# A new head, load order and matmul order for a gated SSM/FFN mix on one Trainium2 core

## The chip, the cores and the metric

The program runs on one core of a Trainium2 chip. A core has five engines that run their own instruction queues and meet only through semaphores: TensorE (PE in the profile, with PEld for its weight loads), VectorE (DVE), ScalarE (ACT), GpSimd (POOL) and SyncE (SP), which here issues nearly all DMAs. Matmul results land in eight PSUM banks. The metric is the device time of one execution in microseconds (us), lower being better. Three executions of the kernel before took 150.77, 152.63 and 154.89 us (median 152.63).

## The reference

Everything is computed for one sequence of 2048 tokens with 448 features, in bf16:

```
g   = sigmoid(sum(x * gate_w))                       # one gate per token
# branch a: a diagonal complex state-space layer, 448 states
dt  = exp(log_dt);  L = exp(dt * (Lambda_re + i Lambda_im))
Bu  = x @ (((L - 1) / Lambda)[:, None] * B).T        # complex
h_t = L * h_{t-1} + Bu_t                             # over 2048 steps
a   = 2 * Re(h @ C.T) + x * Dskip
# branch b: a feed-forward layer, 448 -> 1792 -> 448
b   = silu(x @ w1) @ w2
out = g * a + (1 - g) * b
```

## The kernel before

**Tiling.** The 2048 tokens are cut into 4 stretches of 512 (`tc` = 0 to 3) and 16 blocks of 128 (`tb`). Features are held transposed in `xT` (128 partitions, 4 column blocks; the last block starts at 320, so its upper 64 rows are new). For stretch 0, `xT` is made on TensorE from `xnat` (L409); for the others by transposing DMAs (L365).

**The scan without complex numbers.** Rotating by the phase of each state turns the complex recurrence into a real one with decay `rc`. For each stretch `bu_pair` and `bu_last` give `U` (real and imaginary parts in 7 slots of 128 lanes, with the two halves of slot 3 exchanged into slot 7). `lanes(tc)` is VectorE's part: PA = U·COS, PB = U·SIN (two instructions), PA += PB, then 7 `tensor_tensor_scan` into `Gf` (order of slots 3, 0, 4, 1, 5, 2, 6), each turned into bf16 `Gb` by ScalarE (L636), then Gb·SIN, Gb·COS and their difference `H[tc % 2]`. Six small VectorE instructions (L642 to L646 and `gin`) carry the state on to the next stretch. COS and SIN are tables over 512 positions, made once: GpSimd multiplies positions by `ph` into `Gf` (L464), VectorE takes off the nearest integer (L450, L453), ScalarE computes Sin, Abs and Sin again (L470 to L476), VectorE copies the second half (L478, L479).

**The matmuls.** `F1(tc, k)` is a pair of column blocks of `x @ w1`, `BU(tc, k)` a pair of slots of `Bu`. A pair uses products of 64 rows, two at a time: a "begin" of 8 for the pair, and an "end" of 6, which is issued only after the begin of the next pair (`step`, `close`). So a pair is 14 products and holds 2 banks until its two results are moved out by ScalarE: `aT` (SiLU, L658) or `U` (L587; for stretch 0 half of them by VectorE, L585). `F2(tb)` is 14 products of 128 rows with `w2`, moved out by ScalarE to `Tb` (L672). `C(tb)` is the readout, 7 products of 128 rows of `H` with `CP`, moved out by VectorE to `ot` (L696) after `tf` (L687). `bu_last` (L607) and `gates` (L732) also use 128 rows, and so do the transposes of `B` into `BT` (L533) and of `C` (`readout_weights`, L709).

**What sets the order.** TensorE runs in the order in which the source calls `F1`, `BU`, `F2`, `C` and the rest. For the other engines a planner (`Plan.order`) picks at each point the instruction that can start first by written-down costs, and by `prio` (lower first) among those that can start at once; it also gives out the banks. The result is one fixed list for each engine: an instruction that waits holds up all behind it on its engine.

**DMAs on SP, in order:** x of stretch 0, four pieces of B, three of w1, the transposing loads of stretch 1, w2, four pieces of C, the transposing loads of stretches 2 and 3, Dskip, x of stretches 1 to 3; then the exchanges of slot 3 (`swapped`) and the results.

Of the kernel before, what the change touches and what calls it, by code (L numbers as in the profile page):

```python
# [46 lines left out]
class Plan:  # L47
# [54 lines left out]
    def order(self):  # L102
# [28 lines left out]
        while len(done) < len(ops):  # L131
# [20 lines left out]
            if o.sem is not None:  # L152
                free[o.eng] = t + 0.35
                pipe = max(pipe, t + 1.5) + o.bytes / 260e3
                o.end = pipe + 0.4
            else:
                extra = 0.0
                if o.eng == "pe":
                    extra = self.SWITCH if o.rows != rows else 0.0
                    rows = o.rows  # L160
                free[o.eng] = o.end = t + o.cost + extra
# [3 lines left out]
            for tk in o.ps_w:  # L165
                b = min((x for x in range(8) if holder[x] is None), key=lambda x: (banks[x], x))
                tk.bank = b
                tk.left = tk.users
                holder[b] = tk
# [88 lines left out]
def bass_gated_mix__ssm_conv_s5__dense_activation_silu__prompt_kernel(nc, A_x, A_Lambda_re, A_Lambda_im, A_B_re, A_B_im, A_C_re, A_C_im,  # L258
               A_log_dt, A_Dskip, B_x, B_w1, B_w2, gate_w, out):
    with ExitStack() as ctx:  # L260
# [64 lines left out]
        def sem():  # L325
            _s[0] += 1
            return E(nc.semaphore(name=f"d{_s[0]}"))
# [22 lines left out]
        def load(q, dst, src, name, nbytes, prio):  # L350
            P.add(q, lambda e: e.dma_start(dst, src), [], [name], 0.3, prio, sem(), nbytes)
# [5 lines left out]
        def load_x(tc, prio):  # L357
            load("sp", xnat[:, 4 * tc:4 * tc + 4, :], x2[tc * CH:(tc + 1) * CH, :].rearrange("(b p) d -> p b d", p=128),
                 f"xn{tc}", CH * 896, prio)

        def load_xt(tc, n, prio):

            rows = slice(tc * CH, (tc + n) * CH)
            for k, (o, c) in enumerate(((slice(0, 3), slice(0, 384)), (slice(3, 4), slice(320, 448)))):
                P.add("sp", lambda e, o=o, c=c: e.dma_start_transpose(xT[:, o, rows], x2[rows, c]), [],  # L365
                      [f"xT{t}{k}" for t in range(tc, tc + n)], 1.2, prio + k, sem(), n * CH * (1100, 500)[k])
# [3 lines left out]
        load("sp", Bnat[0:64, 3, :], A_B_re[384:448, :], "Bn1", 64 * 896, 2)  # L370
        load("sp", Bnat[64:128, 3, :], A_B_im[384:448, :], "Bn2", 64 * 896, 3)
        load("sp", Bnat[:, 4:7, :], A_B_im[0:384, :].rearrange("(p s) d -> p s d", s=3), "Bn3", 384 * 896, 4)
        load("sp", w1s[:, 0:3, :], B_w1[0:384, :].rearrange("(b p) f -> p b f", p=128), "w1a", 384 * 3000, 5)
        load("sp", w1s[0:64, 3, 0:896], B_w1[320:384, 0:896], "w1b", 64 * 1500, 6)
        load("sp", w1s[64:128, 3, :], B_w1[384:448, :], "w1c", 64 * 3000, 7)
        load_xt(1, 1, 8)
        load("sp", w2s[:, :, :], B_w2.rearrange("(fb p) d -> p fb d", p=128), "w2", F_FF * 896, 10)
# [4 lines left out]
        load_xt(2, 2, 16)  # L382
        load("sp", dsk[:, :],
             A_Dskip.rearrange("(o n) -> o n", o=1).partition_broadcast(128).rearrange("p o n -> p (o n)"),
             "dsk", 128 * 896, 18)
        for tc in range(1, NCH):
            load_x(tc, 18 + tc)
# [14 lines left out]
        for n, blocks in enumerate(((0, 1), (2, 3))):  # L402
            tk = Ps()

            def mm(pe, tk=tk, blocks=blocks):
                for q, i in enumerate(blocks):
                    for b in range(4):
                        o = (q * 4 + b) * 128
                        r = pe.transpose(bk16(tk)[:, o:o + 128], xnat[:, b, XCOL[i]:XCOL[i] + 128], ident[:, :])  # L409
                return r  # L410
            P.add("pe", mm, ["xn0", "ident"], [tk], 0.6)
            dst = xT[:, blocks[0]:blocks[0] + 2, 0:CH]
            src = lambda tk=tk: bk16(tk)[:, :].rearrange("p (q n) -> p q n", q=2)
            if n == 0:
                DVE(lambda e, src=src, dst=dst: e.tensor_copy(dst, src()), [tk], ["xT00"], 0.7, 2)
            else:
                ACT(lambda e, src=src, dst=dst: e.activation(dst, src(), AF.Copy), [tk], ["xT01"], act_cost(1024), 1)

        def xr(tc):
            return [f"xT{tc}{k}" for k in range(2)]  # L420
# [38 lines left out]
        FR = [Gf[:, 2 * h:2 * h + 2, :] for h in range(2)]  # L459
        wk = [Gf[:, 4, :], Gf[:, 5, :]]  # L460
        for b in range(4):
            h, q = b // 2, b % 2
            dst = Gf[:, b, :]
            POOL(lambda e, b=b, dst=dst: e.tensor_single_scalar(dst, itf[:, :], ph[:, b:b + 1], ALU.mult),  # L464
                 ["itf", "ph"], [f"Gf{b}"], 0.65)
            DVE(nearest(wk[q], dst), [f"Gf{b}"], [f"Gf{4 + q}"], dve_cost(512, 2), 3)
            DVE(minus(dst, dst, wk[q]), [f"Gf{b}", f"Gf{4 + q}"], [f"Gf{b}"], dve_cost(512), 3)
        for h in range(2):
            n = 2 if h == 0 else 1
            ACT(lambda e, h=h, n=n: e.activation(SIN[:, 2 * h:2 * h + n, :], Gf[:, 2 * h:2 * h + n, :], AF.Sin, scale=TURN),  # L470
                [f"Gf{2 * h + k}" for k in range(n)] + ["tbl"], [f"SIN{2 * h + k}" for k in range(n)], act_cost(n * 512), 5)
            if h == 1:
                ACT(lambda e: e.activation(SIN[:, 3, :], Gf[:, 3, :], AF.Sin, scale=sturn[:, :]),  # L473
                    ["Gf3", "sturn", "tbl"], ["SIN3"], act_cost(512, 1), 5)
            ACT(lambda e, h=h: e.activation(FR[h], FR[h], AF.Abs), ["tbl"], [f"Gf{2 * h}", f"Gf{2 * h + 1}"], act_cost(1024), 5)
            ACT(lambda e, h=h: e.activation(COS[:, 2 * h:2 * h + 2, :], FR[h], AF.Sin, bias=hpi[:, :], scale=-TURN),  # L476
                [f"Gf{2 * h}", f"Gf{2 * h + 1}", "hpi", "tbl"], [f"COS{2 * h}", f"COS{2 * h + 1}"], act_cost(1024, 1), 5)
# [45 lines left out]
        def b_transposes(slots, reads, h, to_act):  # L523
# [15 lines left out]
            if to_act:  # L539
                ACT(lambda e: e.activation(dst, src(), AF.Copy), [tk], [name], act_cost(256 * n), 2)  # L540
            else:
                DVE(lambda e: e.tensor_copy(dst, src()), [tk], [name], 0.1 + 0.00058 * 256 * n, 2)

        RE, LAST, IM = (0, 1, 2), (3,), (4, 5, 6)
        b_transposes(RE, ["Bn0"], 0, False)
        b_transposes(RE, ["Bn0"], 1, True)
        bre = ["BT0_0", "BT1_0"]
        bim = ["BT0_4", "BT1_4"]
        b3 = ["BT0_3", "BT1_3", "BT3z"]
# [39 lines left out]
        def bu_pair(tc, k):  # L589
            sa, sb_ = ((0, 1), (4, 2), (5, 6))[k]  # L590
# [4 lines left out]
            return BT, tc, 128 * sa, 128 * sb_, (bre, bre + bim, bim)[k], evict  # L595

        def swapped(t, tn, prio):
            for k, (p, q) in enumerate(((0, 64), (64, 0))):
                P.add("sp", lambda e, p=p, q=q: e.dma_start(t[p:p + 64, 7, :], t[q:q + 64, 3, :]),
                      [f"{tn}3"], [f"{tn}7{'ab'[k]}"], 0.3, prio, sem(), 65536)  # L600

        def bu_last(tc):
# [7 lines left out]
            P.add("pe", mm, b3 + xr(tc), [tk], 0.87)  # L610
# [11 lines left out]
        def lanes(tc):  # L622
# [16 lines left out]
            if tc + 1 < NCH:  # L639
                last = Gf[:, :, CH - 1]  # L640
                gfn = [f"Gf{s}" for s in range(7)]
                DVE(lambda e: e.tensor_tensor(k1[:, :], last, CC[:, :], ALU.mult), gfn + ["CC"], ["k1"], 0.2, pr)  # L642
                DVE(lambda e: e.tensor_tensor(k2[:, 0:3], Gf[:, 4:7, CH - 1], SS[:, 0:3], ALU.mult), gfn + ["SS"], ["k2a"], 0.2, pr)
                DVE(lambda e: e.tensor_tensor(k2[:, 4:7], Gf[:, 0:3, CH - 1], SS[:, 4:7], ALU.mult), gfn + ["SS"], ["k2b"], 0.2, pr)
                DVE(lambda e: e.tensor_tensor(k2[0:64, 3:4], Gf[64:128, 3, CH - 1:CH], SX[64:128, :], ALU.mult), gfn + ["SX"], ["k2c"], 0.2, pr)
                DVE(lambda e: e.tensor_tensor(k2[64:128, 3:4], Gf[0:64, 3, CH - 1:CH], SX[0:64, :], ALU.mult), gfn + ["SX"], ["k2d"], 0.2, pr)  # L646
                DVE(minus(gin[:, :], k1[:, :], k2[:, :]), ["k1", "k2a", "k2b", "k2c", "k2d"], ["gin"], 0.2, pr)
# [7 lines left out]
        def ffn1_pair(tc, k):  # L655
# [4 lines left out]
            return w1s, tc, 128 * k, 896 + 128 * k, ["w1a", "w1b", "w1c"], evict  # L660
# [21 lines left out]
        def readout(tb):  # L682
# [16 lines left out]
            P.add("sp", lambda e: e.dma_start(out2[t0:t0 + 128, :], ot[tb % 3][:, :]), [f"ot{tb % 3}"], [], 0.3, 1,  # L699
# [59 lines left out]
        b_transposes(LAST, ["Bn1", "Bn2"], 0, False)  # L759
        b_transposes(LAST, ["Bn1", "Bn2"], 1, False)  # L760
        DVE(lambda e: e.memset(BT[0:64, 3, 384:512], 0.0), ["BT1_3"], ["BT3z"], 0.2, 2)
        b_transposes(IM, ["Bn3"], 0, False)
        b_transposes(IM, ["Bn3"], 1, True)
# [5 lines left out]
        F1(1, 0)  # L769
        gates(1)  # L770
        lanes(0)
        skip(0)
        F1(1, 1)
        F2(0, 1)
        BU(1, 0)
        bu_last(1)
        BU(1, 1, 2)
        F1(1, 2)
        readout_weights(0)
        readout_weights(1)  # L780
        F2(2)
        F1(1, 3, 4)
        readout_weights(2)
        readout_weights(3)
        F2(3)
        F1(1, 5, 6)
        lanes(1)
        skip(1)
        BU(2, 0)
        gates(2)  # L790
        gates(3)
        bu_last(2)
        BU(2, 1, 2)
        F1(2, 0)
        F2(4)
        C(0, 1)
        F2(5)
        F1(2, 1, 2, 3)
        C(2, 3)
        F2(6, 7)  # L800
# [3 lines left out]
        F1(2, 4)  # L804
        BU(3, 0)
        bu_last(3)
        BU(3, 1, 2)
        F1(2, 5, 6)
        F1(3, 0)
        F2(8)  # L810
        C(4, 5)
        F2(9)
        F1(3, 1, 2, 3)
        F2(10)
        C(6, 7)
        F2(11)
        F1(3, 4, 5, 6)
        lanes(3)
        close()
        C(8, 9, 10, 11)  # L820
        F2(12, 13, 14, 15)
# [36 lines left out]
```

## Time and profile before

| What | us |
|---|---|
| median of three executions | 152.63 |
| the profiled execution itself | 152.47 |
| its span (first to last instruction) | 150.4 |
| PE busy / DVE busy / ACT busy / POOL busy | 139.3 / 123.3 / 83.6 / 21.7 |
| first matmul (transposes of x) | 4.17 |
| first pair of BU(0, 0) begins | 8.86 |
| first F1 begins | 16.33 |
| first PA = U·COS begins on VectorE | 31.33 |
| last matmul of the chain ends | 147.53 |

The span is 2.07 us shorter than the time of the same execution; what lies around it is start and end of the program. The profile lists for each engine the busy time, for each group of instructions their mean duration, and for idle time the instruction that ended it. The chain that ended last is followed back from the last instruction. A busy PE need not be a fast PE: the duration of a matmul record has some pipeline time in it, so costs of matmuls are read here as the distance from one group to the next in the chain, divided by the number of matmuls.

### The profile page before, as it was taken

How to read it: one execution, taken by the hardware profiler on the slowest of the kernel's cores; microseconds unless marked ns; L12 is line 12 of the kernel's file. 1: busy time of each engine (PE TensorE's matmuls, PEld its weight loads, DVE VectorE, ACT ScalarE, POOL GpSimd, SP SyncE). 2: the span in 40 equal slices, each digit the busy share in tenths (PEclk: the TensorE clock that was granted, in tenths of full speed). 3: DMA queues.
4: the chain of work that ended last, by engine and by line, in shares of the span. 5: the costliest groups of instructions: out<-in, count | busy, mean ns of one | idle time of the engine just before them, and what ended most of it. 6: DMA issues, size and time to landing. Idle time of an engine off the chain costs nothing.

```text
span 150.4 us, 2663 instructions
## 1 busy us (share of the span) xinstructions
PE 139.3 (93%) x1055; PEld 68.0 (45%) x1059; DVE 123.3 (82%) x153; ACT 83.6 (56%) x153; POOL 21.7 (14%) x52
## 2 busy tenths in 40 slices
PE   0877999999999999999999999969999999999992
PEld 0734454454345544445445534435445444555450
DVE  0359935089999998998998999998999998799772
ACT  3272999871897768576282156894163069241300
POOL 7189930040000000730000000000000000000000
PEclk9999999999999999999999999999999999999999
DMA  4999999974110000001200000010100001210012
GB/s 159 305 294 183 287 318 128 199 238 165 35 39 2 0 0 4 20 15 35 65 0 31 31 0 25 14 35 0 61 4 0 31 31 35 65 61 2 0 45 80
DMA packets 16644, 11.43 MB, mean 76 GB/s; under 512 B 7924, under 2 KB 15928, under 8 KB 16632
## 3 DMA queue, kind: packets, MB, share of 16 engines
q1 hardware_dynamic: 16624, 11.27, 30.1%
q8 instruction: 8, 0.13, 0.4%
q14 instruction: 4, 0.03, 0.1%
q10 hardware_dynamic: 8, 0.00, 0.0%
HBM read 6.94 MB, written 1.84 MB: 58 GB/s over the span
## 4 chain that ended last, share of the span: by engine, by line
PE 87%; ACT 4%; DVE 4%; DMA 2%; issue 1%; DVEq 0%
PE ps L558 40%; PE ps L668 25%; PE ps L693 14%; DMA xnat<-in_A_x_dram 2%; PE ps L607 2%; PE ps L533 2%; DVE H L620 1%; DVE PA L620 1%; PE ps L409 1%; ACT aT L658 1%; PE ps L709 1%; PE ps L732 1%; ACT BT L540 1%; ACT Gb L636 1%; DVE ot L696 0%
## 5 line engine op out<-in xcount | busy, mean ns | idle before, releaser
L668 PE MATMUL ps<-w2s,aT 128*128 128x448 bf16 x224 | 44.2, 353 | 1.2 <-ACT aT L658 1.2
L558 PE MATMUL ps<-xT,w1s 64*128 64x512 bf16 x392 | 45.0, 376 | 0.0
L658 ACT ACTIVATE aT<-ps 128x512 bf16<-128x512 f32 x56 | 30.3, 596 | 8.0 <-PE ps L558 8.0
L668 PEld LDWEIGHTS ps<-w2s,aT 128*128 128x128 bf16 x224 | 21.5, 98 | 22.3 <-ACT aT L658 2.1
L558 PEld LDWEIGHTS ps<-xT,w1s 64*128 64x128 bf16 x392 | 18.5, 94 | 23.5 <-issue 2.2
L672 ACT ACTIVATE Tb<-ps,g 128x448 bf16<-128x448 f32 x16 | 10.1, 633 | 33.1 <-PE ps L668 31.3
L633 DVE TENSOR_TENSOR_SCAN Gf<-rc,gin,PA 128x512 f32<-128x512 f32 x21 | 25.2, 1262 | 0.0
L558 PE MATMUL ps<-xT,BT 64*128 64x512 bf16 x168 | 21.0, 388 | 2.0 <-ACT BT L540 1.0
L693 PE MATMUL ps<-CP,H 128*128 128x448 bf16 x112 | 22.2, 353 | 0.2 <-DVE H L620 0.2
L636 ACT ACTIVATE Gb<-Gf 128x512 bf16<-128x512 f32 x28 | 17.1, 630 | 4.5 <-DVE Gf L633 4.4
L587 ACT ACTIVATE U<-ps 128x512 bf16<-128x512 f32 x25 | 14.3, 596 | 6.1 <-PE ps L558 5.6
L693 PEld LDWEIGHTS ps<-CP,H 128*128 128x128 bf16 x112 | 10.7, 98 | 11.2 <-DVE H L620 0.7
L696 DVE SCALAR_TENSOR_TENSOR ot<-ps,g,tf 128x448 bf16<-128x448 f32 x16 | 10.9, 683 | 5.8 <-PE ps L693 5.2
L558 PEld LDWEIGHTS ps<-xT,BT 64*128 64x128 bf16 x168 | 8.2, 95 | 12.6 <-DVE phk L450 1.2
L687 DVE SCALAR_TENSOR_TENSOR tf<-xnat,g,Tb 128x448 f32<-128x448 bf16 x16 | 10.6, 678 | 0.5 <-ACT Tb L672 0.3
L738 POOL TENSOR_SCALAR g<-th 128x4 f32<-128x4 f32 x4 | 4.3, 1064 | 39.0 <-ACT th L737 39.0
L620 DVE TENSOR_TENSOR PB<-U,SIN 128x2048 bf16<-128x2048 bf16 (+1 forms) x8 | 8.4, 1085 | 1.3 <-ACT SIN L473 1.3
L620 DVE TENSOR_TENSOR PB<-Gb,SIN 128x1536 bf16<-128x1536 bf16 (+1 forms) x8 | 8.6, 1080 | 0.1
L620 DVE TENSOR_TENSOR H<-PA,PB 128x3584 bf16<-128x3584 bf16 x4 | 8.1, 2024 | 0.1
L620 DVE TENSOR_TENSOR PA<-U,COS 128x3584 bf16<-128x3584 bf16 x4 | 8.1, 2023 | 0.1
L620 DVE TENSOR_TENSOR PA<-PA,PB 128x3584 bf16<-128x3584 bf16 x4 | 8.1, 2024 | 0.1
L620 DVE TENSOR_TENSOR PA<-Gb,COS 128x3584 bf16<-128x3584 bf16 x4 | 8.1, 2018 | 0.0
(92 smaller groups left out, 92.5 us busy)
## 6 DMA issues: line engine op xcount, KB each, us to landing
xnat<-in_A_x_dram SPq DMA_DIRECT2D x4, 448.0 KB, 5.0
out_dram<-ot SPq DMA_DIRECT2D x16, 112.0 KB, 1.7
w2s<-in_B_w_dram SPq DMA_DIRECT2D x1, 1568.0 KB, 10.0
w1s<-in_B_w_dram SPq DMA_DIRECT2D x1, 1344.0 KB, 9.1
Gb<-Gb SPq DMA_DIRECT2D x8, 64.0 KB, 1.9
Tb<-in_A_C_re_dram SPq DMA_DIRECT2D x1, 392.0 KB, 10.4
U<-U SPq DMA_DIRECT2D x6, 64.0 KB, 2.0
Tb<-in_A_B_re_dram SPq DMA_DIRECT2D x1, 336.0 KB, 4.0
```

Of the source, the lines that this page charges most:

```text
L558: r = pe.matmul(bk(tk), w[p0:p0 + 64, k, c0:c0 + 128], xT[p0:p0 + 64, k, xc:xc + CH], start=(start and i == 0), stop=(not start and i == 2))
L587: ACT(lambda e: e.activation(U[:, s, :], bk(tk), AF.Copy), [tk], [f"U{s}"], act_cost(512), 4)
L620: return DVE(lambda e: e.tensor_tensor(o, a, b, op), r, w, dve_cost(n, 2), prio)
L633: DVE(lambda e, s=s, b=b, init=init: e.tensor_tensor_scan(Gf[:, s, :], rc[:, b:b + 1].to_broadcast([128, CH]), PA[:, s, :], init, ALU.mult ...
L636: ACT(lambda e, s=s: e.activation(Gb[:, s, :], Gf[:, s, :], AF.Copy), [f"Gf{s}"], [f"Gb{s}"], act_cost(512), 4)
L658: ACT(lambda e, tk=tk, fb=fb: e.activation(aT[tc % 2][:, fb, :], bk(tk), AF.Silu), [tk, "tbl"], [f"aT{tc % 2}_{fb}"], act_cost(512), 3)
L668: r = pe.matmul(bk(tk)[:, 0:D_MOD], aT[tc % 2][:, fb, o:o + 128], w2s[:, fb, :], start=(fb == 0), stop=(fb == NFB - 1))
L672: ACT(lambda e, tk=tk: e.activation(Tb[:, tb, :], bk(tk)[:, 0:D_MOD], AF.Copy, scale=g1[:, tb:tb + 1]), [tk, f"g1_{tc}"], [f"Tb{tb}"] + [f ...
L687: DVE(lambda e: e.scalar_tensor_tensor(tf[tb % 2][:, :], xnat[:, tb, :], g[:, tb:tb + 1], Tb[:, tb, :], ALU.mult, ALU.add), [f"xn{tc}", f" ...
L693: r = pe.matmul(bk(tk)[:, 0:D_MOD], Ht[:, s, o:o + 128], CP[:, s, :], start=(s == 0), stop=(s == NSLOT - 1))
L696: DVE(lambda e, tk=tk: e.scalar_tensor_tensor(ot[tb % 3][:, :], bk(tk)[:, 0:D_MOD], g[:, tb:tb + 1], tf[tb % 2][:, :], ALU.mult, ALU.add), ...
L738: POOL(lambda e: e.tensor_scalar(g[:, c], th[:, c], 0.5, 0.5, ALU.mult, ALU.add), [f"th{tc}"], [f"g_{tc}"], 0.2, 9)
```

## The change

- **Head.** VectorE zeroes part of `PB`, and TensorE multiplies it by itself 15 times (256 columns each) before the transposes of x, and twice more between two groups of B transposes. Nobody reads the results. `xT` of stretch 0 is moved out in three pieces instead of two. B is transposed in slot groups (0, 1), (4, 5, 6) and (2, 3) instead of (0, 1, 2), (3) and (4, 5, 6), and the pairs of BU are (0, 1), (4, 5), (6, 2) instead of (0, 1), (4, 2), (5, 6).
- **Loads.** The second large piece of B comes second. w1 comes in ten pieces: the columns for k < 3 first, then the rest. w2 goes ahead of the transposing loads of stretch 1. The transposing loads of stretches 2 and 3, Dskip and the later x wait for the exchange of `Gb` slot 3 of stretch 0.
- **Tables.** ScalarE instead of GpSimd makes two of the four blocks of `Gf`; Abs moves from ScalarE to VectorE (as max(x, -x)); the Sin instructions get `prio` 2, ahead of SiLU's 3.
- **Carries.** Four of the six small instructions for each stretch move from VectorE to GpSimd.
- **Phases.** In each stretch all pairs of 64 rows come together, and then all work of 128 rows; C and F2 alternate block by block. Before, the two kinds changed 25 times from 13.31 us on; in the new order they change 11 times from the first pair on.
- The planner's costs for DMA issue and its bookkeeping of banks are altered too, which changes the lists of ScalarE and VectorE.

```diff
         load("sp", Bnat[:, 0:3, :], A_B_re[0:384, :].rearrange("(p s) d -> p s d", s=3), "Bn0", 384 * 896, 1)
-        load("sp", Bnat[0:64, 3, :], A_B_re[384:448, :], "Bn1", 64 * 896, 2)
-        load("sp", Bnat[64:128, 3, :], A_B_im[384:448, :], "Bn2", 64 * 896, 3)
-        load("sp", Bnat[:, 4:7, :], A_B_im[0:384, :].rearrange("(p s) d -> p s d", s=3), "Bn3", 384 * 896, 4)
-        load("sp", w1s[:, 0:3, :], B_w1[0:384, :].rearrange("(b p) f -> p b f", p=128), "w1a", 384 * 3000, 5)
-        load("sp", w1s[0:64, 3, 0:896], B_w1[320:384, 0:896], "w1b", 64 * 1500, 6)
-        load("sp", w1s[64:128, 3, :], B_w1[384:448, :], "w1c", 64 * 3000, 7)
-        load_xt(1, 1, 8)
-        load("sp", w2s[:, :, :], B_w2.rearrange("(fb p) d -> p fb d", p=128), "w2", F_FF * 896, 10)
+        load("sp", Bnat[:, 4:7, :], A_B_im[0:384, :].rearrange("(p s) d -> p s d", s=3), "Bn3", 384 * 896, 2)
+        load("sp", Bnat[0:64, 3, :], A_B_re[384:448, :], "Bn1", 64 * 896, 3)
+        load("sp", Bnat[64:128, 3, :], A_B_im[384:448, :], "Bn2", 64 * 896, 4)
+        for h, (c0, c1) in enumerate(((0, 384), (384, 896))):
+            w = w1s[:, :, :].rearrange("p b (q f) -> p b q f", q=2)
+            for b in range(3):
+                load("sp", w[:, b, :, c0:c1], B_w1[128 * b:128 * b + 128, :].rearrange("p (q f) -> p q f", q=2)[:, :, c0:c1],
+                     f"w1{h}{b}", 128 * 4 * (c1 - c0), 5 + h)
...
+        load("sp", w2s[:, :, :], B_w2.rearrange("(fb p) d -> p fb d", p=128), "w2", F_FF * 896, 8)
+        load_xt(1, 1, 9, (3.0, 5.0))
...
-        load_xt(2, 2, 16)
...
+        def late_loads():
+            load_xt(2, 2, 16, (6.0, 1.4), ["Gb7a", "Gb7b"])
...
+        DVE(lambda e: e.memset(PB[:, 0, :], 0.0), [], ["PB0"], 0.2, 0)
+
+        def idle(n):
+            tk = Ps()
...
+                for _ in range(n):
+                    r = pe.matmul(ps[:, tk.bank, 0:256], PB[:, 0, 0:128], PB[:, 0, 0:256], start=True, stop=True)
+                return r
+            P.add("pe", mm, ["PB0"], [tk], 0.107 * n)
+
+        idle(15)
...
-                ACT(lambda e, src=src, dst=dst: e.activation(dst, src(), AF.Copy), [tk], ["xT01"], act_cost(1024), 1)
+                ACT(lambda e: e.activation(xT[:, 2, 0:CH], bk16(tk)[:, 0:CH], AF.Copy), [tk], ["xT01"], act_cost(512), 1)
+                DVE(lambda e: e.tensor_copy(xT[:, 3, 0:CH], bk16(tk)[:, CH:2 * CH]), [tk, "xT01"], ["xT02"], 0.42, 2)
...
+            if b < 2:
+                ACT(lambda e, b=b, dst=dst: e.activation(dst, itf[:, :], AF.Copy, scale=ph[:, b:b + 1]),
+                    ["itf", "ph"], [f"Gf{b}"], act_cost(512, 1), 2)
+            else:
+                POOL(lambda e, b=b, dst=dst: e.tensor_single_scalar(dst, itf[:, :], ph[:, b:b + 1], ALU.mult),
+                     ["itf", "ph"], [f"Gf{b}"], 1.65)
...
-            ACT(lambda e, h=h: e.activation(FR[h], FR[h], AF.Abs), ["tbl"], [f"Gf{2 * h}", f"Gf{2 * h + 1}"], act_cost(1024), 5)
...
-                [f"Gf{2 * h + k}" for k in range(n)] + ["tbl"], [f"SIN{2 * h + k}" for k in range(n)], act_cost(n * 512), 5)
+                    frn + ["tbl"], ["SIN0", "SIN1"], act_cost(1024), 2)
...
+            DVE(lambda e, fr=fr: e.scalar_tensor_tensor(fr, fr, -1.0, fr, ALU.mult, ALU.max), [], frn, dve_cost(1024), 3)
+            ACT(lambda e, h=h, fr=fr: e.activation(COS[:, 2 * h:2 * h + 2, :], fr, AF.Sin, bias=hpi[:, :], scale=-TURN),
+                frn + ["hpi", "tbl"], [f"COS{2 * h}", f"COS{2 * h + 1}"], act_cost(1024, 1), 2)
...
+        B01, B23, B456 = (0, 1), (2, 3), (4, 5, 6)
+        b_transposes(B01, ["Bn0"], 0, False)
+        b_transposes(B01, ["Bn0"], 1, True)
+        idle(2)
+        b_transposes(B456, ["Bn3"], 0, False)
+        b_transposes(B456, ["Bn3"], 1, True)
...
-            sa, sb_ = ((0, 1), (4, 2), (5, 6))[k]
+            sa, sb_ = ((0, 1), (4, 5), (6, 2))[k]
...
-                DVE(minus(gin[:, :], k1[:, :], k2[:, :]), ["k1", "k2a", "k2b", "k2c", "k2d"], ["gin"], 0.2, pr)
+                POOL(minus(gin[:, :], k1[:, :], k2[:, :]), ["k1", "k2a", "k2b", "k2c", "k2d"], ["gin"], 0.2, pr)
```

The order of TensorE's work after the change, from the first pair on (`close()` issues the end of the last open pair):

```
BU(0, 0); b_transposes(B23); BU(0, 1, 2); F1(0, 0); bu_last(0); gates(0); F1(0, 1..6)
lanes(0); late_loads(); skip(0); F1(1, 0, 1, 2); close()
F2(0); bu_last(1)
BU(1, 0, 1, 2); F1(1, 3, 4, 5, 6); close()
gates(1); readout_weights(0), (1); F2(1); readout_weights(2), (3); F2(2, 3); lanes(1); skip(1)
BU(2, 0, 1, 2); F1(2, 0..6); close()
bu_last(2); gates(2); gates(3); C(0); F2(4); C(1); F2(5); C(2); F2(6); C(3); F2(7); lanes(2); skip(2); skip(3)
BU(3, 0, 1, 2); F1(3, 0..6); close()
bu_last(3); C(4); F2(8); C(5); F2(9); C(6); F2(10); C(7); F2(11); lanes(3)
F2(12); C(8); F2(13); C(9); F2(14); C(10); F2(15); C(11); C(12, 13, 14, 15)
```

## The prediction

> **What bounds the kernel now.** I read the page's 40 slices first, to see which engines are full and when.
>
> ```profile
> PE   0877999999999999999999999969999999999992
> DVE  0359935089999998998998999998999998799772
> ACT  3272999871897768576282156894163069241300
> DMA  4999999974110000001200000010100001210012
> ```
>
> PE is full from the fourth slice on (a slice is 3.76 us), DVE only from the ninth. DMA is full for 33 us and then nearly empty. PEclk stands at 9 throughout, so this profile reports no throttle. Next, the chain that ended last, in order of time (start, duration, what):
>
> ```profile
> 4.17 1.89 PE ps L409 x16
> ...
> 8.86 1.89 PE ps L558 x8
> 10.76 1.58 PE ps L533 x16
> ...
> 13.31 4.71 PE ps L558 x42
> ...
> 19.37 10.68 PE ps L558 x98
> ...
> 32.15 5.40 PE ps L668 x28
> ...
> 44.78 0.90 PE ps L709 x16
> 45.68 2.65 PE ps L668 x14
> ...
> 99.09 0.60 ACT aT L658
> ```
>
> It is matmuls almost without a break from 13.31 on, and it has the prices: a product of 64 rows takes 10.68/98 = 0.109 us, F2 2.65, C 1.325 (28 products in 5.30), a transpose 0.056 (0.90/16). Early ones cost double: the first pair 1.89/8 = 0.236 each, the transposes of x 0.118. A change between 64 and 128 rows costs 0.1 (the F2 at 32.15 took 5.40, not 5.30). Last, VectorE in order of time and the waits, because the slices show it joining late:
>
> ```profile
> DVE COS L478 <- ACT COS L476: 5.9, 1, 5.9
> ```
> ```profile
> 30.73 0.56 DVE L478 COPY COS<-COS 128x1536 bf16<-128x1536 bf16 x1 [5.89 <-ACT COS L476]
> 31.33 2.03 DVE L620 TENSOR_TENSOR PA<-U,COS 128x3584 bf16<-128x3584 bf16 x1
> ...
> 139.96 2.02 DVE L620 TENSOR_TENSOR H<-PA,PB 128x3584 bf16<-128x3584 bf16 x1
> ```
>
> VectorE waits 5.89 us for the cosine tables, which ScalarE makes between SiLUs, then works almost without pause until H of the last stretch at 141.98. PE's last F2 ends at 141.83, and the final C needs that H. So **two bounds meet within 0.2 us at the end**: matmuls, and VectorE's chain. A change must shorten both to gain.
>
> **PE's sum.** 560 products of 64 rows x 0.109 = 61.0; 16 F2 = 42.4; 16 C = 21.2; 4 bu_last at 0.87 = 3.5; gates and readout weights 8 x 0.45 = 3.6. Together 131.7. Test on before: less the first begin (0.87), plus 25 changes of rows (2.5) and the 1.1 by which ScalarE holds PE between 95.56 and 99.74 (4.18 us for 28 products worth 3.05), that is 134.4; measured are 147.53 - 13.31 = 134.2. After: 11 changes instead of 25, so 1.1 instead of 2.5.
>
> **The head, step by step.** (1) The zero products: I take twice the price at full rate of 256 columns, 0.213 (as a 128-column transpose's step is 0.107 early); 15 are 3.2 us, from about 1.05 (zeroing PB is a VectorE write beside nothing; 0.11 to 0.56 by the smallest and the 1536-column copy, I take 0.3) to 4.25, and x lands at 4.12 (issued 0.73, 3.39 to landing). Nothing real waits for them but 0.1 us. (2) What they may buy is full rate for the head. In before, 28 transposes from 4.17 to 7.87 left the step at 0.107; it fell to 0.056 at 11.9, 3.0 us after the first real products at 8.86, and the 1.2 us gap after that did not undo it. Zero products for 3.2 us should do the same by 4.3 to 5. Bounds: no effect, or full. I take full, being the nearest in length.
> [...]
> (3) Full-rate path: 16 transposes to 5.2; parameters and B (0, 1) to 6.6; two zero products and 12 transposes to 7.5, while VectorE (0.69, 0.16, 0.4, 0.17, 0.4) and ScalarE (0.6, 0.6) empty the banks by 7.4. The first BU begins at 7.6, against 8.86. (4) All B transposes but one group are then done. The second table load (1.28, after dtc and rc, from 8.7) ends at 10.0, and the last BT copy behind it at 10.65: PE waits 0.3. F1(0, 0) begins at 12.2, against 16.33. (5) w1's first part must be there. SP reaches its five issues by 6.3 (0.5 to 0.6 each); the DMAs move 240 to 330 GB/s, so 0.72 MB behind x and B lands at about 9.5, or 11 if pieces of 768 bytes are slower than those of 3584. Covered. The second part (0.96 MB more, 13 to 14) is wanted at 18.3.
>
> **The tables.** Gf of two blocks on ScalarE (0.63 by Gb, 0.72 by the scaled Sin) end at 11.9. VectorE then passes U copies (0.69 each), nearest and minus (0.43, 0.62) and two max(x, -x) over 1024 columns. That instruction is not in the trace: 1.05 by ScalarE's Abs, 1.5 by two minus; I take 1.25. It also waits, in its queue, for U3 of bu_last (15.5). So Sin runs from 15.6, the first Cos at 18.5, the second at 22.0 to 23.1, the COS copy ends at 24.0, and **lanes(0)'s PA begins at about 24 instead of 31.33**. The price is on ScalarE: tables and 4 SiLU pairs in one stretch, some 9 us of work against 7.3 us of PE. With 8 banks and 2 per pair PE is held when two pairs are unemptied, at F1(0, 5) and F1(0, 6): I count 0.8 us.
>
> **xT of stretch 1** now queues behind ten w1 issues and w2. Its own issues took 2.98 and 5.16 us on SP; from 9.6 they end at 17.8, and landing came 2 us after the last. The DMAs need about 17 for w2 and 4 to 5 more for these: 20 to 22.5. F1(1, 0) wants it at 24.4. Covered by 2 us. The later transposes are behind the Gb exchange (31 to 33): issued 6 us, landing 8.8 after issue, 41 to 45; wanted at 54. The U exchange of stretch 1 is queued behind them on SP: 41; VectorE wants it at 45.
>
> **VectorE's chain.** From PA to the last H it took 110.65, with 4.6 of waits. Two tf and two ot (0.6 each) move behind H, 12 small carries leave (0.1 each): 102.5 of work. From 24 that is 127; with the waits now in its queue for C(4) to C(9) I get H at 132.5. The final C comes on PE at 135 to 136. So VectorE drops out as a bound by about 3 us, and the fewer instructions there gain nothing themselves. The carries on GpSimd cost 0.19 (alone) to 1.97 each (the gates' beside VectorE): 0.8 to 8 us per stretch, between the last scan (36.5) and the next first scan (54): hidden. In the long stretches of 64 rows ScalarE has 20 moves of 0.54 and 7 Gb of 0.55, 14.7, in 15.3 of PE; by banks I find 0.2 us of holds, and leave them out.
>
> **The sum.** 7.6 + 131.7 + 8 transposes 0.45 + 11 changes 1.1 + table wait 0.3 + ScalarE hold 0.8 = 141.95 for PE's end, against 147.53. Behind it stands what stood there before (last ot, its DMA): 150.4 - 147.53 = 2.87. Span 144.8, the execution's time 2.07 more: 146.9 against 152.47. The median lies 0.16 above that profiled execution, so **147.0**.
>
> **Rivals.**
> - *The rate stays low in the head* (0.22). For: transposes alone did not raise it. Against: the zeros are products, for as long as it took. First BU at 8.9, its begin 1.89, B (2, 3) 0.95, from 11.75 on the same 130.8, plus 1.6 of changes and holds: PE's end 144.1, time 149.2.
> - *xT of stretch 1 is late* (0.13). w2 took 10.0 us from issue and these transposes 9.7; one fully after the other, from 9.0, gives 28.7. Every us past 25.2 is a us of PE: +3.5, 150.5. Against: in before those transposes shared the DMAs with w1 and landed 2 us behind it.
> - *The tables come no earlier, and ScalarE's list stops PE* (0.07, slower). Its list now has Gb of lanes(0) between SiLUs of F1(1, 0) to F1(1, 2) and the U of stretch 1. If PA still begins at 31.3, the first scan ends at 36.6 instead of 29.3; behind that wait stand four SiLUs, PE fills its last banks at BU(1, 1) and each following Gb delays a U: PE loses about 7, time 154. It decides from a PA at about 26. For: VectorE's list has waits for U3 and three table results in a row. Against: each of their prices is in the trace, and none is 2 us.
> - *It does not fill* (0.06): many small holds, +1 to 3.
>
> **Chances.** The forecast has 0.52, with its own range 145.5 (no hold, nothing at the table load) to 148 (an extra us in holds). The range to the rivals: 145.0 to 151.0. A measurement of this kernel can tell about 2% from no change. Faster by over 2% is under 149.6: the forecast, most of the first rival, some of the others, 0.76; within 2%: 0.19; slower by over 2%: 0.05.
>
> **What would show it.** Zero products ending at 4.2 to 4.3 and transposes of x with a step of 0.056; F1(0, 0) at 12 to 12.5; no wait of VectorE for COS above 1 us and PA at 23 to 25; PE without a gap over 0.5 us from 25 to 141, with C(12) not waiting for H. I am wrong if PE waits at F1(1, 0) for a DMA, if PA begins after 26, or if the transposes of x still step at 0.107.

## The result and the profile after

Four executions of the changed kernel took 145.11, 145.66, 145.87 and 146.12 us (median 145.76), beside a median of 152.43 for the kernel before. The ratio is 0.959, with a 95% interval from 0.951 to 0.968: **faster by 4.1%**. The forecast was 147.0, with a range from 145.0 to 151.0. (Ratios here leave out executions over 1.5% above the fastest of the same kernel, of which the kernel before has many, so a ratio is not always the quotient of the medians beside it.)

The profiled execution is the one of 145.11. Its span is 143.3, and its slices are 3.58 us long:

```profile
PE   6899999999999999999999999999999999999991
DVE  0459979999999999999799999969479999889592
```

PE is at work from the first slice on (those are the zeros) and full from the third. VectorE is full from the fourth, and its dips near 100 us (the 6 and the second 4) and near 135 us (the second 5) are deeper than any that it had in the middle of its row before: it has slack there now. The chain that ended last (start, duration, what):

```profile
1.18 3.29 PE ps L420 x15
4.46 0.91 PE ps L435 x16
...
7.61 0.97 PE ps L595 x8
...
21.55 1.05 ACT COS L512
22.60 0.49 ACT aT L695
23.09 0.05 issue
23.14 6.87 PE ps L595 x62
...
133.85 6.63 PE ps L731 x35
```

The transposes of x (L435) now step at 0.91/16 = 0.057 instead of 0.118, and the first BU costs 0.97 for 8 instead of 1.89. What is new is the piece from 14.8 to 23.1: there the chain leaves PE and runs over ScalarE and VectorE, through U, the tables and six SiLUs, and it is ScalarE that lets PE go on at 23.14. From there to 140.48 the chain is PE alone.

The old head also had two waits of 0.99 us, for what ScalarE makes, in front of the products of BU. The profile before shows them as

```profile
8.86 1.89 PE L558 MATMUL ps<-xT,BT 64*128 64x512 bf16 x8 [0.99 <-ACT rc L446]
...
13.31 3.20 PE L558 MATMUL ps<-xT,BT 64*128 64x512 bf16 x28 [0.99 <-ACT BT L540]
```

and in the changed kernel neither is there:

```profile
7.55 1.04 PE L595 MATMUL ps<-xT,BT 64*128 64x512 bf16 x8
...
9.07 3.23 PE L595 MATMUL ps<-xT,BT 64*128 64x512 bf16 x28
```

VectorE in order of time:

```profile
23.34 0.55 DVE L514 COPY COS<-COS 128x1536 bf16<-128x1536 bf16 x1
23.92 2.03 DVE L657 TENSOR_TENSOR PA<-U,COS 128x3584 bf16<-128x3584 bf16 x1
...
130.39 2.02 DVE L657 TENSOR_TENSOR H<-PA,PB 128x3584 bf16<-128x3584 bf16 x1
```

PA begins at 23.92 instead of 31.33, without a wait for COS, and the last H is done at 132.41, while the first C that needs it comes at 135.2 (after the seven products of C(11), at 133.85). So VectorE has 2.8 us to spare, and PE alone is the bound.

### The profile page after: what moved, and what is told of

The parts are those of the page before. It is cut to its first block, busy times and chain, and to the rows that moved or that the text cites. A ratio compares the mean times of both kernels' runs of the same rounds, so it can differ in the third digit from the quotient of the medians.

```text
span 143.3 us, 2726 instructions
## 1 busy us (share of the span) xinstructions
PE 138.5 (97%) x1076; PEld 69.3 (48%) x1076; DVE 123.9 (86%) x144; ACT 82.6 (58%) x154; POOL 25.3 (18%) x62
## 4 chain that ended last, share of the span: by engine, by line
PE 91%; ACT 5%; DVE 2%; issue 0%; DVEq 0%
PE ps L595 37%; PE ps L706 30%; PE ps L731 15%; PE ps L644 3%; PE ps L420 2%; ACT aT L695 2%; ACT COS L512 1%; PE ps L569 1%; PE ps L747 1%; PE ps L770 1%; PE ps L435 1%; DVE Gf L482 0%; DVE ot L734 0%; ACT SIN L507 0%; DVE U L653 0%
## 5 line engine op out<-in xcount | busy, mean ns | idle before, releaser
L706 PE MATMUL ps<-w2s,aT 128*128 128x448 bf16 x224 | 44.7, 353 | 0.0
L595 PE MATMUL ps<-xT,w1s 64*128 64x512 bf16 x392 | 43.8, 376 | 0.3 <-ACT aT L695 0.3
L695 ACT ACTIVATE aT<-ps 128x512 bf16<-128x512 f32 x56 | 29.6, 598 | 5.1 <-PE ps L595 5.1
L670 DVE TENSOR_TENSOR_SCAN Gf<-rc,gin,PA 128x512 f32<-128x512 f32 x21 | 25.8, 1269 | 0.0
L731 PE MATMUL ps<-CP,H 128*128 128x448 bf16 x112 | 23.1, 353 | 0.0
L595 PE MATMUL ps<-xT,BT 64*128 64x512 bf16 x168 | 19.7, 377 | 0.0
L679 POOL TENSOR_TENSOR k<-Gf,CC 128x7 f32<-128x7 f32 x3 | 2.8, 927 | 50.5 <-DVE Gf L670 50.5
```

Source lines behind the costliest of these rows:

```text
L595: r = pe.matmul(bk(tk), w[p0:p0 + 64, k, c0:c0 + 128], xT[p0:p0 + 64, k, xc:xc + CH], start=(start and i == 0), stop=(not start and i == 2))
L670: DVE(lambda e, s=s, b=b, init=init: e.tensor_tensor_scan(Gf[:, s, :], rc[:, b:b + 1].to_broadcast([128, CH]), PA[:, s, :], init, ALU.mult ...
L695: ACT(lambda e, tk=tk, fb=fb: e.activation(aT[tc % 2][:, fb, :], bk(tk), AF.Silu), [tk, "tbl"], [f"aT{tc % 2}_{fb}"], act_cost(512), 3)
L706: r = pe.matmul(bk(tk)[:, 0:D_MOD], aT[tc % 2][:, fb, o:o + 128], w2s[:, fb, :], start=(fb == 0), stop=(fb == NFB - 1))
L731: r = pe.matmul(bk(tk)[:, 0:D_MOD], Ht[:, s, o:o + 128], CP[:, s, :], start=(s == 0), stop=(s == NSLOT - 1))
```

## The experiments

e1 to e7 and e11 take one part out of the changed kernel, e12 alters it in three places, and e8 to e10 put one part into the old one. Each time is a median, and each ratio is taken beside the kernel before on the same chip; the changed kernel itself was timed apart from them. Executions of one kernel lie 0.2 to 1.4 us apart near 146 us, so medians that differ by less than about 1 us are not told apart here.

### The zeros: e1, e2, e3 and e9

e1 leaves out all 17 zero products:

```diff
-        idle(15)
...
-        idle(2)
```

> The changed kernel without any product of zeros. Theory (the zeros bring the matmul rate up early, and PE is the bound to the end): x transposes step at 0.107 us again, the first BU begins at about 8.9, the rate rises about 3 us after that, and PE's end moves by about 2.1 us: 147.9 against 145.8. Rival (the new head is faster by its order alone, zeros are idle decoration): first BU at 7.6, time 145.8.

**Measured:** 146.26 (145.71 to 147.08), ratio 0.965 [0.952, 0.977]: 0.5 us more than with the zeros by the medians, not 2. The profile is that of the fastest of its four executions (145.71). PE in order of time in it:

```profile
3.85 1.89 PE L434 MATMUL ps<-ident,xnat 128*128 128x128 bf16 x16 [3.85 <-DMA xnat<-in_A_x_dram]
...
6.09 1.79 PE L568 MATMUL ps<-ident,Tb 128*128 128x128 bf16 x20
7.90 1.04 PE L593 MATMUL ps<-xT,BT 64*128 64x512 bf16 x8
```

The transposes of x are slow (1.89), but the rate rises among the transposes of B: the 20 of them take 1.79, where 16 at the low rate take 1.89 and 8 at the full rate 0.62 (the 8 from 8.87 on). By that the step goes from 0.107 to 0.056 at about 7.2, and the first BU is at full rate (1.04), without the old head's wait of 0.99. **Here transposes alone came before the rise**, 3.4 us of them. They do not always do it: in the kernel before, e8 and e10, which have no zeros either, the same 3.7 us of transposes (from about 4 to 7.9) left the first BU at half rate (1.89). The rest is later by 0.3: PA at 24.25, PE's end at 140.80. How the head ran in the three longer executions (up to 147.08) is not known.

e2 leaves out the two in the middle alone:

```diff
-        idle(2)
```

> The changed kernel without the two products of zeros between the B transposes; the 15 at the start stay. Theory (the rate, once up, holds through 3 us of transposes): no transpose steps at 0.107, and the 0.22 us that the two take on PE's chain are won: 145.6. [...]

**Measured:** 145.55 (145.18 to 145.69), ratio 0.959 [0.950, 0.968]. The two zero products in the middle make no difference that can be told apart.

e3 makes fewer at the start:

```diff
-        idle(15)
+        idle(8)
```

> 8 products of zeros at the start instead of 15: 1.7 us of work that ends at 2.9, then 1.2 us without any until x lands. Theory (the rate rises after some 3 us of nearly unbroken products): x transposes step at 0.107, the rate rises only after the first BU, time 147 to 147.9. Rival (any burst of products is enough): x transposes at 0.056, time 145.8.

**Measured:** 147.19 (146.64 to 147.40), ratio 0.970 [0.960, 0.980]: the highest median of the three. Its executions overlap with those of e1 (146.64 is below two of e1's), so it is not shown that eight zeros are worse than none. Eight zeros end 0.77 us before x lands, and in this profile, which is that of the longest execution (147.40), the low rate stays far longer than in e1's:

```profile
8.75 1.66 PE L595 MATMUL ps<-xT,BT 64*128 64x512 bf16 x8
10.34 0.62 PE L569 MATMUL ps<-ident,Tb 128*128 128x128 bf16 x8
```

The first BU takes 1.66, and only the transposes behind it are fast. The first F1 begins at 13.93 instead of 12.12, and PE ends 1.8 us later. That is the slow head which the prediction's first rival described, near the 2.1 us that it was priced at.

e9 puts the 15 zeros into the kernel before, with the bookkeeping of banks that goes with them:

```diff
+        DVE(lambda e: e.memset(PB[:, 0, :], 0.0), [], ["PB0"], 0.2, 0)
+        idle_tk = Ps()
+
+        def idle_mm(pe):
+            for _ in range(15):
+                r = pe.matmul(ps[:, idle_tk.bank, 0:256], PB[:, 0, 0:128], PB[:, 0, 0:256], start=True, stop=True)
+            return r
+        P.add("pe", idle_mm, ["PB0"], [idle_tk], 0.107 * 15)
```

> The kernel before with the 15 products of zeros at the start alone. Theory: the head of PE shortens by about 2.5 us (first BU at 7.9, full rate), and ScalarE's list, in which the tables stand between SiLUs, moves with it, so that VectorE's PA moves to 29 to 30: time 150 to 150.5. Rival (VectorE's chain is the bound and its start is set by GpSimd and ScalarE, not by PE): PA still at 31, 152.

**Measured:** 150.67, ratio 0.980 [0.973, 0.987]. Its four executions lie between 150.60 and 150.90, while 13 of the kernel before on the same chip lie between 150.92 and 155.03. The best executions of the kernel before, on this and the other chips, take 150.65 to 150.92 too. **So in these runs the zeros bring every execution near the best time and take away the spread**, which is worth more to the kernel before than to the changed one, whose executions with the zeros still lie 1.0 us apart (1.4 without, e1). That the spread comes from the rate in the head fits the profiles below and was not tested further. The zeros move both bounds at once: PA begins at 29.50 instead of 31.33, as expected, and the end of PE moves by as much, from 147.53 to 145.69, still behind H:

```profile
138.13 2.04 DVE H L631
140.16 0.05 issue
140.21 5.48 PE ps L704 x28
```

### Tables and matmul order, one without the other: e5, e8, e10, e6

e5 is the changed kernel with the tables made as before: all of `Gf` on GpSimd, Abs on ScalarE, rank 5. Its core:

```diff
-            DVE(lambda e, fr=fr: e.scalar_tensor_tensor(fr, fr, -1.0, fr, ALU.mult, ALU.max), [], frn, dve_cost(1024), 3)
-            ACT(lambda e, h=h, fr=fr: e.activation(COS[:, 2 * h:2 * h + 2, :], fr, AF.Sin, bias=hpi[:, :], scale=-TURN),
-                frn + ["hpi", "tbl"], [f"COS{2 * h}", f"COS{2 * h + 1}"], act_cost(1024, 1), 2)
+            ACT(lambda e, h=h: e.activation(FR[h], FR[h], AF.Abs), ["tbl"], [f"Gf{2 * h}", f"Gf{2 * h + 1}"], act_cost(1024), 5)
+            ACT(lambda e, h=h: e.activation(COS[:, 2 * h:2 * h + 2, :], FR[h], AF.Sin, bias=hpi[:, :], scale=-TURN),
+                [f"Gf{2 * h}", f"Gf{2 * h + 1}", "hpi", "tbl"], [f"COS{2 * h}", f"COS{2 * h + 1}"], act_cost(1024, 1), 5)
```

> The changed kernel with the old making of the tables (all four Gf blocks on GpSimd, Abs on ScalarE, Sin after SiLU). Theory (late tables hold ScalarE's list and through the banks PE, as the third rival of the prediction priced it): PA of stretch 0 begins at 29 to 31, PE has gaps of 5 to 7 us in all between 30 and 45, time 151 to 153. Rival (VectorE is only late, PE runs on until it needs the last H): no gap in PE before 130, a wait of PE for H at the end of about 4 us, time 149.5. Rival 2 (tables do not matter): 145.8.

**Measured:** 161.29 (158.68 to 162.51), ratio 1.054 [1.040, 1.067]: 15.5 us more than with the new tables by the medians, 13.8 by the executions that the ratios count, and far above the 151 to 153 that were expected. In the profile, of an execution of 162.24, PA begins at 35.5, the last H ends at 149.97, and PE waits for it:

```profile
150.02 7.39 PE L724 MATMUL ps<-CP,H 128*128 128x448 bf16 x28 [7.37 <-DVE H L650]
```

e8 is the kernel before with the new order of matmuls and nothing else. For stretch 2:

```diff
-        BU(2, 0)
+        BU(2, 0, 1, 2)
+        F1(2, 0, 1, 2, 3, 4, 5, 6)
+        close()
+        bu_last(2)
...
-        C(0, 1)
+        C(0)
...
+        C(1)
...
+        C(2)
+        F2(6)
+        C(3)
+        F2(7)
```

> The kernel before with the new order of matmuls alone. Theory (two bounds, and late tables stop PE through ScalarE's list): 14 changes less save 1.4, but PE has gaps of several us between 30 and 50: 152 to 156. Rival (the order of matmuls is the gain): 149 or less.

**Measured:** 160.43 (160.34 to 162.80), ratio 1.059 [1.051, 1.068]: **slower by 8 us**, and 4 above the expected range. PA begins at 31.33 as in the kernel before, H ends at 147.76, and the same wait stands at the end:

```profile
147.82 7.57 PE L693 MATMUL ps<-CP,H 128*128 128x448 bf16 x28 [7.37 <-DVE H L620]
```

The last 28 products, behind the idle 7.37 us, need 7.6 us instead of the 5.5 that they need in e10 (below); the row of the granted clock shows 8, 5, 7 and 9 in the last four slices, from 142.5 on. Had they followed C(11) at once (28 in 5.3), PE's end of 155.4 would be 145.7, which is 1.8 ahead of the kernel before.

e10 is the kernel before with the new tables and nothing else (the edit of e5 the other way):

```diff
-            ACT(lambda e, h=h: e.activation(FR[h], FR[h], AF.Abs), ["tbl"], [f"Gf{2 * h}", f"Gf{2 * h + 1}"], act_cost(1024), 5)
...
+            DVE(lambda e, fr=fr: e.scalar_tensor_tensor(fr, fr, -1.0, fr, ALU.mult, ALU.max), [], frn, dve_cost(1024), 3)
```

> The kernel before with the new making of the tables alone. Theory (two bounds that meet at the end): VectorE's PA begins 4 to 6 us earlier and the final C no longer waits for H, but PE is full from 13.3 on, so that only the hold of 1.1 us near 96 can go: 151 to 152.4. Rival (VectorE's chain was the bound): 146 to 148.

**Measured:** 152.16 (12 executions, 150.94 to 154.13), ratio 1.000 [0.994, 1.006]: nothing. The profile is that of the longest execution. PA begins at 26.60 and the last H ends at 136.10, 5.9 us earlier than in the kernel before (141.98), but the C that needs it comes when PE has got to it, without a wait:

```profile
143.75 5.46 PE L700 MATMUL ps<-CP,H 128*128 128x448 bf16 x28
```

e6 is the changed kernel with the old order (the edit of e8 the other way). For stretch 1:

```diff
-        F1(1, 0, 1, 2)
-        close()
-        F2(0)
+        F1(1, 1)
+        F2(0, 1)
+        BU(1, 0)
...
-        BU(1, 0, 1, 2)
-        F1(1, 3, 4, 5, 6)
-        close()
+        BU(1, 1, 2)
+        F1(1, 2)
```

> The changed kernel with the old order of matmuls after the head (25 changes between 64 and 128 rows instead of 11). Theory: 14 changes at 0.1 us, and 0 to 1 us of holds by ScalarE: 147.2 to 148.2. Rival (the regrouping is where most of the 6.7 us came from): 150 or more. Rival 2 (a change of rows costs nothing): 145.8.

**Measured:** 148.82 (148.52 to 148.96), ratio 0.983 [0.975, 0.992]: the new order is worth 3.1 us where the tables are early. The last `ot` begins 3.0 later. Of that, 14 changes between 64 and 128 rows at 0.1 would be 1.4, and the hold that the kernel before has at an F2 (at 99.74 there) is back:

```profile
96.10 2.82 PE L706 MATMUL ps<-w2s,aT 128*128 128x448 bf16 x14 [1.18 <-ACT aT L695]
```

The two parts therefore depend on each other:

| Head, loads, carries | Order | Old tables | New tables |
|---|---|---|---|
| old | old | 152.43 (before) | 152.16 (e10) |
| old | new | 160.43 (e8) | not run |
| new | old | not run | 148.82 (e6) |
| new | new | 161.29 (e5) | 145.76 (after) |

e10 and e6 both have the new tables and the old order, so the 3.3 us between them (2.6 by their ratios) belong to the head, the loads, the carries and the planner's altered costs together. Of these, the zeros (e1), the carries (e4) and the loads (e7), taken out one by one, each move the median by 0.5 or less. What is left would fall to the new grouping of B and xT and to the planner's costs, which no run takes out alone; that the two waits of 0.99 us in the old head are gone, with zeros and without (e1), fits this.

### How much of the tables is their rank: e11

```diff
-                    frn + ["tbl"], ["SIN0", "SIN1"], act_cost(1024), 2)
+                    frn + ["tbl"], ["SIN0", "SIN1"], act_cost(1024), 5)
...
-                frn + ["hpi", "tbl"], [f"COS{2 * h}", f"COS{2 * h + 1}"], act_cost(1024, 1), 2)
+                frn + ["hpi", "tbl"], [f"COS{2 * h}", f"COS{2 * h + 1}"], act_cost(1024, 1), 5)
```

> The changed kernel with only the planner's rank of the Sin and Cos instructions put back behind SiLU (5 instead of 2); how they are made stays new. The second Cos then stands in ScalarE's list behind the SiLUs of F1(1, 0) instead of those of F1(0, 2), so PA of stretch 0 should begin at 28 to 29, about 5 us late. Theory (what matters is when the tables are ready, and VectorE has about 3 us to spare before PE is held or the last C waits): 1 to 4 us lost, 147 to 150. Rival 1 (what cost the old tables 15 us was the work on ScalarE and GpSimd, not the place in the list): 145.8. Rival 2 (every us of PA past 24 costs more than one, as the old tables suggest with 15 us for 11.6): 151 or more.

**Measured:** 157.42 (157.29 to 158.25), ratio 1.038 [1.032, 1.045]: most of the loss of e5, by the rank alone, as its second rival had it and not the theory. ScalarE's Sins stand behind SiLUs, and VectorE waits for them:

```profile
25.16 1.22 DVE L511 SCALAR_TENSOR_TENSOR Gf<-Gf 128x1024 f32<-128x1024 f32 x1 [5.30 <-ACT SIN L509]
...
30.05 0.56 DVE L514 COPY COS<-COS 128x1536 bf16<-128x1536 bf16 x1 [1.66 <-ACT COS L512]
```

PA begins at 30.64, 6.7 us later than in the changed kernel, but the time is 11.7 us longer. The difference is at the end:

```profile
135.40 1.49 PE L731 MATMUL ps<-CP,H 128*128 128x448 bf16 x7
144.25 7.73 PE L731 MATMUL ps<-CP,H 128*128 128x448 bf16 x28 [7.37 <-DVE H L657]
```

C(11) itself begins only 1.7 us later than in the changed kernel (135.40, not 133.68), 1.53 of it by one hold of ScalarE at 59.86. The wait is 7.37, and the last 28 products lose 2.4 against an unbroken row. VectorE's list in that time:

```profile
136.92 0.69 DVE L734 SCALAR_TENSOR_TENSOR ot<-ps,g,tf 128x448 bf16<-128x448 f32 x1 [0.33 <-PE ps L731]
137.52 0.95 DVE L657 TENSOR_TENSOR PB<-Gb,SIN 128x1536 bf16<-128x1536 bf16 x1
138.39 0.68 DVE L725 SCALAR_TENSOR_TENSOR tf<-xnat,g,Tb 128x448 f32<-128x448 bf16 x1
138.98 1.22 DVE L657 TENSOR_TENSOR PB<-Gb,SIN 128x2048 bf16<-128x2048 bf16 x1
140.12 2.02 DVE L657 TENSOR_TENSOR PA<-Gb,COS 128x3584 bf16<-128x3584 bf16 x1
142.17 2.03 DVE L657 TENSOR_TENSOR H<-PA,PB 128x3584 bf16<-128x3584 bf16 x1
```

That wait is 7.37 in e5, e8 and e11 alike, whether PA is late by 6.7, 7.4 or 11.6. In all three, VectorE's list has the `ot` of C(11) and then five more instructions, of which H is the last (in e5 the `ot` at 142.69, then the same five, to 149.97). So where these instructions stand behind that `ot`, PE has nothing to do from C(11) to H, and in these three the size of the delay that put them there made no difference. The delay also grows on its way: from PA to the last H VectorE takes 108.5 us in the changed kernel, 113.6 in e11, 114.5 in e5 and 116.4 in e8. Before that H, `ot` waits for PE's C products 3.7 us in the changed kernel, 5.5 in e11, 8.4 in e5 and 8.9 in e8 (the view of waits has 5.9, 10.3, 12.5 and 13.2, of which 2.2, 4.8, 4.1 and 4.3 lie behind it): two engines in step, each held by the other's list. That is read from the traces; no run took the `ot` out of that place alone.

### What turned out to be worth nothing: e4 and e7

e4 puts the four carries back on VectorE, one of the four lines being

```diff
-                POOL(minus(gin[:, :], k1[:, :], k2[:, :]), ["k1", "k2a", "k2b", "k2c", "k2d"], ["gin"], 0.2, pr)
+                DVE(minus(gin[:, :], k1[:, :], k2[:, :]), ["k1", "k2a", "k2b", "k2c", "k2d"], ["gin"], 0.2, pr)
```

> The changed kernel with all six carry instructions on VectorE as before. Theory (VectorE has slack; the final C does not wait for H): time 145.8, H of the last stretch later by up to 1 us, PE's chain the same. Rival (VectorE's chain still counts): 12 instructions of about 0.1 us and their waits, 147.

**Measured:** 145.76 (145.51 to 145.99), ratio 0.961 [0.949, 0.974]: the same median as with them on GpSimd. H ends at 132.47 instead of 132.41.

In e7 the three large pieces of w1 replace the ten, and the transposing loads of stretch 1 stand ahead of w2 again:

```diff
...
+        load("sp", w1s[:, 0:3, :], B_w1[0:384, :].rearrange("(b p) f -> p b f", p=128), "w1a", 384 * 3000, 5)
+        load("sp", w1s[0:64, 3, 0:896], B_w1[320:384, 0:896], "w1b", 64 * 1500, 6)
+        load("sp", w1s[64:128, 3, :], B_w1[384:448, :], "w1c", 64 * 3000, 7)
+        load_xt(1, 1, 8, (3.0, 5.0))
```

> The changed kernel with w1 in three pieces and the transposing loads of stretch 1 ahead of w2 again. Theory: w1 lands at 12.8 to 13.7 as in the kernel before, F1(0, 0) is wanted at 12.1, PE waits 1 to 1.6 us for it: 147 to 147.4. Rival (covered, since ScalarE's tables hold PE a little later anyway): 145.8 to 146.1.

**Measured:** 145.40 (145.32 to 145.53), ratio 0.960 [0.954, 0.967]. The new loads gain nothing, against the expected wait of 1 to 1.6 us without them: PE's first F1 and F1(1, 0) find their data in both orders.

### A version that keeps what helps: e12

The changed kernel with the loads of e7, without the two zeros of e2, and with the last readout block in two halves of 224 columns, each with its own `ot` and DMA:

```diff
+            for q in range(2 if tb == NTB - 1 else 1):
+                lo, hi = ((0, 224), (224, 448))[q] if tb == NTB - 1 else (0, 448)
...
+                        r = pe.matmul(bk(tk)[:, lo:hi], Ht[:, s, o:o + 128], CP[:, s, lo:hi], start=(s == 0), stop=(s == NSLOT - 1))
```

> The changed kernel with the old loads of w1 and the old place of the transposing loads, without the two middle products of zeros, and with the last readout block cut into two halves of 224 columns, each with its own ot and DMA. Theory: loads and middle zeros cost nothing or 0.2, the half ot at the end is 0.3 shorter: 145.0 to 145.3 against 145.8. Rival (a DMA of 448-byte rows lands later, or the second DMA queues behind the first): 145.4 to 145.8.

**Measured:** 144.91 (six executions, 144.90 to 145.22), ratio 0.955 [0.950, 0.960]. The last `ot` takes 0.45 instead of 0.68. The lowest median of all, 0.85 us under the changed kernel's (0.6%); the intervals of the two ratios overlap.

## Why the prediction was right, and where it was not

The forecast lay 1.2 us above the median, which is inside the forecast's own range (145.5 to 148). Its steps, beside the profiled execution (the fastest of the four, 0.65 under the median):

| Step | Forecast | Measured |
|---|---|---|
| zero products end; step of the transposes of x | 4.25; 0.056 | 4.3; 0.057 |
| first BU, first F1 begin | 7.6, 12.2 | 7.55, 12.12 |
| first part of w1 landed | 9.5 to 11 | 9.7 |
| xT of stretch 1 landed | 20 to 22.5 | 22.0 |
| PA of stretch 0 | about 24 | 23.92 |
| PE's wait for the second table load | 0.3 | none |
| ScalarE holds PE in F1(0, 5), F1(0, 6) | 0.8 | 0.32 |
| last H ends; first C that needs it | 132.5; 135 to 136 | 132.41; 135.2 |
| PE's end, tail behind it, around the span | 141.95, 2.87, 2.07 | 140.48, 2.8, 1.8 |

**Two bounds at once: right, and the core of it.** The prediction said that matmuls and VectorE's chain meet within 0.2 us at the end, and that a change must shorten both. The runs show it from both sides: the tables alone gain nothing (e10), the order alone costs 8 us (e8, where the prediction's words would lead one to expect no gain, not a loss), and either one without the other in the changed kernel loses 15.5 or 3.1 us (e5, e6). The zeros alone do gain (e9), as they bring both forward. PE's terms held: 98 products of 64 rows in 10.68, F2 2.65, C 1.32 as before.

**The sum was too high by small terms.** PE's end came 1.47 earlier than forecast: 0.3 for the table wait, 0.5 for the hold, 0.3 for gates and readout weights (3.3 in place of 3.6), and 0.4 that stays spread over the changes of rows and the head. Another 0.26 is the time around the span, which was 2.07 in the old profile.

**What failed is a premise in step (2) of the head, and a sign came true by luck.** Step (2) took from the old trace, in which 28 transposes left the step at 0.107, that it takes products to raise the rate, and priced the head without full rate at 2.1 us. e1 contradicts the first half: the rate can rise behind transposes alone, and the loss without zeros was 0.5 by the medians. The price itself was near right for a head that does stay slow (e3, 1.8 at PE's end), but that no zeros means such a head was wrong. Nor do 15 zeros make sure of full rate by 4.3 to 5: of nine profiles with them, the transposes of x ran at full rate in three (the changed kernel with 1.06 for 16, e6 with 1.09, and e4), sped up midway in one (e11, 1.62) and stayed slow in five (e2, e5, e7, e9, e12: 1.91). The step of 0.057 in the table was therefore a lucky draw. It costs little when it fails: in the slow ones with the new head the first BU begins at 8.05 to 8.31 instead of 7.55.

The runs give no fixed distance for the rise. It came 3.4 us after the first transpose in e1, and in the profiles with 15 zeros between 3.0 us (the changed kernel) and 6.0 us (e5) after the first zero product, although those two heads issue the same matmuls up to there. What sets the place is not shown.

**The third rival had the place wrong and the price too low.** It gave 154 for tables that come no earlier, with PE stopped by ScalarE's list from BU(1, 1) on, for about 7 us. e11 (PA at 30.64) took 157.4, e5 (PA at 35.5) 161.3, and at BU(1, 1) PE waits for nothing in e11 and only 0.30 right behind it in e5. ScalarE holds it one stretch later, before F1(2, 0), by 1.53 and 3.25 us. The terms that the rival lacks are the wait of 7.37 us that forms behind C(11), and 2.1 to 2.4 us of low rate after it. Its condition, a PA after about 26, was not tested in the new order between 25.8 (e3, where PE is late too) and 30.6. The chance given to it (0.07) rested on prices of single waits in the trace, and these held: the wait of VectorE for the third Sin was 0.84, and none of the table waits was 2 us.

**What it called covered was covered.** Loads (e7), carries (e4) and the two middle zeros (e2) each moved the median by less than 0.4 us, which the runs can't tell from nothing.

## What to carry to other kernels

When two engines end together, a change to either one alone can show nothing or even a loss, so test the parts in pairs before dropping one. In a fixed list, work that stands behind an instruction which waits for another engine can give the delay back with interest at the end (6.7 us became 11.7 in e11), so price a delay by what stands in the list behind it. Dummy products before the first data paid here most by taking away the spread from run to run (e9). Let them last until the data lands: eight that ended 0.8 us too early showed no gain over none (147.19 and 146.26).

## What was not expected of the hardware

- **The rate of the head varied from one profiled execution to the next.** In profiles with 15 zeros the step of the transposes or products fell to full rate at 4.2 to 7.2 us; with eight by 10.3; without, at 7.2 (e1), 11.9 (before), between 12.2 and 13.3 (e8) and at about 17 (e10). The last three have the same old head with the same two breaks of 1.0 us. In e10, the 28 BU products from 13.54 on still took 5.06 us, and 3.2 is the full-rate time (before). The row of the granted clock shows 9 in all slices of the head in each of these, so the low rate there must be read from the steps.
- **PE was slow after its longest idle times.** After 7.37 us of idle, 28 products took 7.4 to 7.7 us (e5, e8, e11) instead of 5.5 (e10), and after 3.25 us in e5 the next 8 took 1.89 instead of 1.04, while after 1.53 us in e11 they took 1.04. Here the clock's row does fall; e11's has 8, 5 and 8 in its last slices:

```profile
PEclk9999999999999999999999999999999999998589
```

- **Small GpSimd instructions varied much.** In the first stretch of the changed kernel a 128x7 product took 0.83 and the 128x7 difference behind it 1.20 us, and 128x3 products 0.19, all in the same 3 us; in the next two stretches that same difference took 1.04 and 0.20. On VectorE each takes 0.15 to 0.16 (e4). The cause was not looked for. Since the result is there at 38.6, far ahead of 53.3, where it is wanted, that cost nothing.
